# Attention scores in three single PSUM tiles, transposes in three banks

## The chip, the core and the metric

The kernel runs on one core of one Trainium2 chip. A core has a matrix engine (PE, with its weight loads, PEld), a vector engine (DVE), a scalar engine (ACT), a general engine (POOL) and queues that start transfers (SP, and POOL's own). PE writes its results into PSUM, which has eight banks; a bank holds 512 float32 numbers in each of 128 partitions, and DVE and ACT read them from there. The metric is the time on the device for one execution, in microseconds; lower is better.

## The reference

Eight batches with eight heads of 64 numbers each: 512 local and 32 global tokens. Local queries see the local keys within a window of 32 to either side, and all global keys; global queries see all keys. The result of the attention is the input of a layer of eight experts, where each token goes to one expert.

```python
s_g = scale * np.matmul(q_g, k_all.transpose(0, 1, 3, 2))
out_g = np.matmul(sm(s_g), v_all)
s_ll = np.where(mask, scale * np.matmul(q_l, k_l.transpose(0, 1, 3, 2)), -1e9)
s_l = np.concatenate([s_lg, s_ll], axis=-1)
out_l = np.matmul(sm(s_l), np.concatenate([v_g, v_l], axis=2))
...
expert_idx = np.argmax(logits, axis=1)
h = np.maximum(x[mask] @ w1[e], 0.0)
out[mask] = gate_w[mask, None] * (h @ w2[e])
```

## The kernel before

The kernel has an attention part, which also routes each token to its expert and scatters its row into a buffer in device memory (`xs`), and an expert part, which works through items of 128 rows of one expert.

**The attention part** is cut into steps, five for each batch. A batch has four *units* of 128 local queries (`unit`) and one *globals* piece of work (`globals_`). A unit is spread over three steps:

- `scores` (step t): 16 or 32 products of queries and keys (L439 for paired units, in which two heads' halves share a product; L443 for the others). On the chip each product is two instructions, so a unit is 32 instructions of L439 or 64 of L443. They fill two banks of PSUM, `s_ps[0]` and `s_ps[1]`, with four blocks k of 128 columns each. Then DVE reads the blocks, the two banks in turn (k = 0 of one, k = 0 of the other, and so on, L450): it adds the mask, writes the sum to `pb` and keeps the row maximum in `nm`. ACT takes the exponential of each block (L455). So there are eight reads and eight exponentials of 128x128 for a unit.
- `turn` (step t + 1): for each of two halves a tile `pt` (one bank) takes four transposes of `pb` (L463), and ACT copies it to `pT` (L464).
- `values` (step t + 2): 32 products with the values into the tile `po` (L474), and DVE's division by the row sum (L397 to L399, `quotients`) into `xt`, the attention's output.

The globals do the same with 544 keys in two parts (`scores(0, ...)` and `scores(1, ...)`, L513, L518, read by DVE in L529), then `turn` (L549 to L554) and `values` (L564).

The routing (`route`) works on the finished rows: it transposes them into `pt` tiles (`turn`, L594, copied by ACT in L596), multiplies with the experts' vectors (`logits`, L616, copied in L617 to `us`), transposes back (`back`, L635), finds the expert and the row's place (`choose`, `gates`, `place`, L687 to L709), and scatters the rows with indirect transfers on POOL's queue (`send`, L716).

**Buffers.** PSUM's eight banks in this part are three pools: `ps_s` for the scores (two tiles of two banks), `ps_o` for values (one tile of two banks), and `ps_t` for transposes and all the small products of the routing (two tiles of one bank, name `pt`). A pool hands its tiles out in turn; the first writer of a tile waits until the last reader of what lay there before is done. When the attention part is over, the pools are closed, and the expert part has four pools of its own over the same banks.

**Order.** The first steps (before step 2) and the last ones (from step 40) run in the order in which they are written. Between them a planner orders each engine's instructions when the program is built: among those whose inputs, by its own reckoning, are there and whose tile is free, it takes the one that is written first. What comes out of it is a fixed order on each engine, which the chip keeps to.

**Loads.** SP starts the transfers of queries, keys (`raw`) and values (`vt`) for the next batch, each tied to an instruction of the attention (`mark`, `paced`).

**The early block.** At the end of the attention two blocks of 128 rows of expert 0 are worked through outside of the items (`early_block`); the first of them runs between the last attention steps, takes its intermediate tiles (L154, L168) from `ps_s` and its last one (L181) from `ps_o`, both through short functions that hand out a tile (`acc`, `acc2`).

## Time and profile before

| | |
|---|---|
| median of 3 runs | 757.07 us (756.87 to 760.34) |
| the profiled execution: time | 755.93 us |
| the profiled execution: span from first to last instruction | 754.1 us |
| attention part | up to about 265 us |
| granted TensorE clock over the span | 0.993 |

The profile is that of one execution. In a list of groups, a row names the line, the engine, the operation, output and inputs by the names in the program, the shape and the count. In the timeline, a row is a run of like instructions: its start, its length, and in brackets the idle time of the engine before it with what ended it. In the list of waits, a row names who waited, for whom, the total, the number of times and the longest. "issue" stands where the profile shows nothing that the engine waited for. A wait for several things is put down to the one that came last by the profile.

### The profile page before, as it was taken

The numbers are of one execution on the slowest core, as the hardware profiler recorded it, in microseconds if no ns is written. First come the engines' busy times: TensorE is split into PE (matmuls) and PEld (weight loads), VectorE is DVE, ScalarE is ACT, GpSimd is POOL, SyncE is SP. The second block draws the span as 40 slices with busy tenths as digits, with TensorE's granted clock in tenths as the row PEclk, the third lists the DMA queues.
The fourth block names the chain that finished last, engine by engine and source line by source line (L and its number), as shares of the span: only waits on it lengthen the run. The fifth ranks groups of instructions, "written<-read, shape, count | busy, mean of one in ns | idle before, by whom it ended". The sixth has DMA issues, their size and how long they took to land.

```text
span 754.1 us, 23074 instructions
## 1 busy us (share of the span) xinstructions
PE 713.8 (95%) x7782; PEld 549.9 (73%) x7782; DVE 407.7 (54%) x1385; ACT 472.5 (63%) x988; POOL 289.2 (38%) x306
## 2 busy tenths in 40 slices
PE   8898998999989999999999999999999999999992
PEld 4576776666758546888888888888888888888882
DVE  2757666776665474454545454545555454544441
ACT  4767676766767545666666656565656565656661
POOL 1121241323312244544444444444444444445451
PEclk9999999999999999999999999999999999999997
DMA  9987878868865469566555556565656565556561
GB/s 290 353 272 244 270 219 254 250 205 272 244 219 170 129 248 328 199 220 209 211 203 217 194 222 209 211 210 210 207 199 218 203 210 204 209 206 218 198 225 65
DMA packets 67850, 166.69 MB, mean 221 GB/s; under 512 B 6532, under 2 KB 20484, under 8 KB 67728
## 3 DMA queue, kind: packets, MB, share of 16 engines
q1 hardware_dynamic: 61968, 147.25, 58.0%
q0 software_dynamic: 5760, 17.87, 6.8%
q8 instruction: 70, 1.15, 0.6%
q14 instruction: 52, 0.43, 0.2%
HBM read 142.49 MB, written 23.65 MB: 220 GB/s over the span
## 4 chain that ended last, share of the span: by engine, by line
PE 81%; ACT 5%; DVE 4%; issue 4%; DMA 3%; SPq 1%; POOL 0%; DVEq 0%; POOLq 0%; ACTq 0%
PE g L1085 18%; PE g L1081 18%; PE g L1080 18%; PE s_ps L439 4%; PE hps L1103 4%; ACT pb L455 4%; PE pt L463 3%; PE po L474 3%; PE pt L594 2%; PE po L564 2%; PE xps L1056 2%; DMA raw<-in_qk_dram 2%; PE s_ps L443 1%; PE s_ps L513 1%; DVE pb L450 1%
## 5 line engine op out<-in xcount | busy, mean ns | idle before, releaser
L1076 DVE TENSOR_TENSOR WL<-stg,WH 128x512 f32 (+1 forms) x144 | 151.9, 1055 | 129.6 <-ACT WH L1074 129.6
L1076 POOL TENSOR_TENSOR WL<-stg,WH 128x512 f32 (+1 forms) x144 | 174.1, 1209 | 93.6 <-ACT WH L1074 92.0
L1074 ACT CAST WH<-stg 128x512 f32 (+1 forms) x288 | 177.4, 618 | 7.0 <-DMA stg<-in_wraw_dram 2.9
L1080 PE MATMUL g<-WH,hH 128*128 (+1 forms) x288 | 120.0, 417 | 0.0
L1080 PE MATMUL g<-WH,xH 128*128 (+1 forms) x288 | 117.3, 407 | 0.0
L1085 PE MATMUL g<-WH,xL 128*128 (+1 forms) x288 | 114.2, 397 | 0.0
L1081 PE MATMUL g<-WL,xH 128*128 (+1 forms) x288 | 114.2, 396 | 0.0
L1081 PE MATMUL g<-WL,hH 128*128 (+1 forms) x288 | 113.9, 396 | 0.0
L455 ACT ACTIVATE pb<-pb,nm 128x128 f32<-128x128 f32 x256 | 78.9, 389 | 43.1 <-DVE nm L450 36.2
L139 POOL DMA_INDIRECT out_dram<-ob x37 | 36.8, 993 | 153.6 <-ACT ob L137 153.6
L1085 PE MATMUL g<-WH,hL 128*128 (+1 forms) x288 | 84.7, 395 | 0.0
L1106 DVE TENSOR_TENSOR hL<-hps,hH 128x512 fp32r<-128x512 f32 x72 | 49.8, 692 | 57.8 <-ACT hH L1105 57.8
L450 DVE CUSTOM_DVE_ANT_0 pb<-s_ps,mask 128x128 f32<-128x128 f32 x256 | 57.6, 285 | 43.3 <-PE s_ps L443 18.7
L716 POOL DMA_INDIRECT xs<-xt,si x32 | 32.0, 1000 | 88.2 <-DVE ss L600 19.9
L1085 PEld LDWEIGHTS g<-WH,hL 128*128 128x128 f32 x288 | 54.4, 189 | 13.1
L1085 PEld LDWEIGHTS g<-WH,xL 128*128 128x128 f32 x288 | 54.1, 188 | 13.0
L1097 ACT ACTIVATE h<-g 128x512 f32<-128x512 f32 x72 | 42.9, 596 | 32.7 <-PE g L1085 32.7
L137 ACT ACTIVATE ob<-g,xr 128x512 f32<-128x512 f32 x36 | 24.7, 687 | 61.1 <-PE g L1085 61.1
L1080 PEld LDWEIGHTS g<-WH,xH 128*128 128x128 f32 x288 | 54.3, 189 | 12.0 <-issue 0.2
L1081 PEld LDWEIGHTS g<-WL,xH 128*128 128x128 f32 x288 | 54.4, 189 | 11.7 <-DVE ob L138 0.2
L420 POOL COPY stg<-raw 64x512 f32<-64x512 f32 x42 | 26.5, 631 | 91.7 <-DMA xs<-xt,si 36.2
L1081 PEld LDWEIGHTS g<-WL,hH 128*128 128x128 f32 x288 | 54.4, 189 | 10.0
(199 smaller groups left out, 1054.8 us busy)
## 6 DMA issues: line engine op xcount, KB each, us to landing
stg<-in_wraw_dram SPq DMA_DIRECT2D x36, 2048.0 KB
vt<-in_va_dram SPq DMA_DIRECT2D x98, 260.0 KB
raw<-in_qk_dram SPq DMA_DIRECT2D x56, 204.0 KB
xr<-xs SPq DMA_DIRECT2D x38, 257.0 KB
raw<-in_qk_dram SPq DMA_DIRECT2D x28, 200.0 KB
xs<-fill SPq DMA_DIRECT2D x9, 514.0 KB
stg<-in_wraw_dram SPq DMA_DIRECT2D x16, 256.0 KB
vt<-in_va_dram SPq DMA_DIRECT2D x4, 520.0 KB
```

Of the source, the lines that this page charges most:

```text
L139: nc.gpsimd.indirect_dma_start(out=out[:, :], out_offset=bass.IndirectOffsetOnAxis(ap=ob[:, DM : DM + 1].bitcast(U32), axis=0), in_=ob[:, ...
L439: nc.tensor.matmul(s_ps[j // 2][rows2(j), cs], qd[:, k, j], ks, start=True, stop=True)
L450: ins = nc.vector.tensor_tensor_reduce(p1, s_ps[grp][:, cs], mask[:, m : m + P], -ISQ, 3.0e38, ALU.add, ALU.min, n1)
L455: nc.scalar.activation(p1, p1, AF.Exp, bias=n1, scale=-1.0)
L716: ins = nc.gpsimd.indirect_dma_start(out=xs[:, :], out_offset=bass.IndirectOffsetOnAxis(ap=st["si"][:, t : t + 1], axis=0), in_=get(t), in ...
L1074: made.append(nc.scalar.copy(WH[:, ds(ra, 1), cs], s3))
L1076: made.append(eng.tensor_tensor(WL[:, ds(r, 1), cs], s3, WH[:, ds(r, 1), cs], ALU.subtract))
L1080: reads.append(nc.tensor.matmul(o.unsqueeze(1), a, WH2[:, ds(rp, 1), sl], start=first, stop=False))
L1081: reads.append(nc.tensor.matmul(o.unsqueeze(1), a, WL2[:, ds(rp, 1), sl], start=False, stop=False))
L1085: reads.append(nc.tensor.matmul(o.unsqueeze(1), a, WH2[:, ds(rp, 1), sl], start=False, stop=last))
L1097: nc.scalar.activation(h[:, nh * 512 : (nh + 1) * 512], g, AF.Relu)
L1106: nc.vector.tensor_tensor(hL[:, nh * 4 : nh * 4 + 4, :].rearrange("p c n -> p (c n)"), hp_, hv, ALU.subtract)
```

## The change

The pool of the scores has three tiles of one bank (it had two tiles of two banks), and the pool of the transposes has three tiles (it had two). A unit, and each part of the globals, takes two single tiles where it took one double tile and split it. The early block takes a single tile where it took the first half of a double one. In all, the attention part has eight banks as before: 3 + 2 + 3 in place of 4 + 2 + 2.

```diff
-        ps_s = actx.enter_context(tc.tile_pool(name="ps_s", bufs=2, space=PSUM))
+        ps_s = actx.enter_context(tc.tile_pool(name="ps_s", bufs=3, space=PSUM))
         ps_o = actx.enter_context(tc.tile_pool(name="ps_o", bufs=1, space=PSUM))
-        ps_t = actx.enter_context(tc.tile_pool(name="ps_t", bufs=2, space=PSUM))
+        ps_t = actx.enter_context(tc.tile_pool(name="ps_t", bufs=3, space=PSUM))
...
             def scores():
                 raw = state["raw", b]
-                s_ps = ps_s.tile([P, 2, 512], F32, name="s_ps")
-                s_ps = [s_ps[:, grp] for grp in range(2)]
+                s_ps = [ps_s.tile([P, 512], F32, name="s_ps") for _ in half]
...
                     st["gm"] = sm.tile([P, 4], F32, name="gm")
-                s_ps = ps_s.tile([P, 2, 512], F32, name="s_ps")
-                s_ps = [s_ps[:, grp] for grp in range(2)]
+                s_ps = [ps_s.tile([P, 512], F32, name="s_ps") for _ in half]
                 kn = 96 * (w1 - w0)
...
-                lambda: ps_s.tile([P, 2, 512], F32, name="s_ps")[:, 0],
+                lambda: ps_s.tile([P, 512], F32, name="s_ps"),
                 lambda: ps_o.tile([P, 2, 512], F32, name="po")[:, 0],
```

## The prediction

> **What bounds the kernel now.** I read the page's table of engines first, then busy time by stretch.

> ```profile
> span 754.1 us, 23074 instructions
> PE 713.8 (95%) x7782; PEld 549.9 (73%) x7782; DVE 407.7 (54%) x1385; ACT 472.5 (63%) x988; POOL 289.2 (38%) x306
> ...
> 20.00:57.00 37.00, 31.96 (x842) 23.45 (x830) 23.97 (x150) 25.14 (x69) 7.27 (x14) 1.00 0.93 310
> 57.00:86.40 29.40, 27.42 (x670) 20.52 (x670) 20.04 (x125) 21.14 (x58) 8.34 (x13) 1.00 0.78 236
> 86.40:115.80 29.40, 27.20 (x670) 20.41 (x670) 20.39 (x125) 21.32 (x58) 9.26 (x14) 1.00 0.84 264
> ...
> 209.00:246.00 37.00, 33.97 (x860) 25.29 (x860) 24.13 (x152) 25.34 (x66) 8.06 (x15) 1.00 0.61 190
> ...
> 286.00:754.00 468.00, 453.77 (x2169) 368.32 (x2167) 227.29 (x291) 284.67 (x506) 210.85 (x181) 0.99 0.59 207
> ```

> The columns of a stretch are its length, then PE, weight loads, DVE, ACT and POOL. The pools that change live only in the attention part, up to some 265 us; the expert items after it have pools of their own. One batch of attention lasts 29.4 us, in which PE is busy 27.2 to 27.4 and ACT and DVE 20 to 21. So PE sets the pace, and the change adds or removes no instruction of it. What it can win is PE's idle time, about 2 us of a batch. The next question is what that idle time waits for: the list of waits of PE, 0 to 290 us (total, times, longest).

> ```profile
> PE s_ps L443 <- issue: 5.7, 6, 1.7
> PE pt L635 <- ACT pT L464: 4.7, 5, 1.1
> PE po L474 <- issue: 2.9, 6, 1.0
> PE s_ps L439 <- issue: 2.3, 1, 2.3
> PE pt L594 <- DVE xt L399: 1.9, 2, 1.2
> ...
> PE po L474 <- DVE nm L450: 1.1, 1, 1.1
> ...
> PE pt L549 <- ACT gT L550: 0.7, 1, 0.7
> ...
> PE pt L616 <- ACT pT L464: 0.5, 1, 0.5
> PE pt L463 <- ACT xT L596: 0.2, 1, 0.2
> ```

> Two things are to be seen. Transposes into `pt` wait for ACT's copies out of other `pt` tiles, 4.7 + 0.7 + 0.5 + 0.2 = 6.1 us in all. And no row has a matmul into `s_ps` waiting for DVE: with four banks the scores never stand behind a read. The rows with "issue" name no releaser, and I leave them as they are on both sides.

> **The change, part by part.**

> *Transposes get a third bank.* This is the wait at its most frequent place, by the timeline:

> ```profile
> 111.66 0.37 ACT L617 COPY us<-pt 128x256 f32<-128x256 f32 x1 [0.28 <-PE pt L616]
> 112.54 1.09 PE L463 MATMUL pt<-ident,pb 128*128 128x128 f32 x8
> 113.09 2.46 ACT L455 ACTIVATE pb<-pb,nm 128x128 f32<-128x128 f32 x8 [1.07 <-DVE nm L450]
> 113.57 1.12 PE L474 MATMUL po<-vt,pT 128*32 128x65 f32 x64
> 114.62 0.68 PE L513 MATMUL s_ps<-raw 64*32 64x288 f32 x6
> 115.20 0.69 DVE L399 TENSOR_TENSOR xt<-po,rs 128x512 f32<-128x512 f32 x1
> 115.46 1.04 ACT L464 COPY pT<-pt 128x512 f32<-128x512 f32 x2
> 116.08 0.66 PE L635 MATMUL pt<-ident,us 128*128 128x128 f32 x4 [0.77 <-ACT pT L464]
> 116.57 0.64 PE L594 MATMUL pt<-ident,xt 128*128 128x128 f32 x4
> 117.14 0.70 PE L513 MATMUL s_ps<-raw 64*32 64x288 f32 x10
> ...
> L464 ACT COPY pT<-pt x64: 559/578/597, 14.9 to 248.2; 128x512 f32<-128x512 f32 x64
> ```

> L463 has filled both banks by 113.63. ACT does eight exponentials (2.46 us) before it copies the first bank out, at 115.46 + 0.58 = 116.04, and L635 starts at 116.08. Its own input `us` was ready at 112.03. With a third bank (the one that L617 emptied at 112.03) L635 runs in the idle time, right behind the six L513. But the L594 behind it still needs the bank that ACT frees at 116.04, and its `xt` is ready only at 115.20 + 0.69 = 115.89; so it starts at about 116.08 in place of 116.57. The gain is 116.57 - 116.08 = 0.49 us at each of the five places, not the whole 0.8 to 1.1 us: 2.45. What is late next is ACT's first copy again. The three single waits have other work behind them and go whole: L616 0.5, L549 0.7, L463 0.2 (that one in the written tail). Together 3.8 us; the ends are 0, where every wait only moves to the next instruction, and 6.1, where all go.

> [...]

> *Scores lose a bank: three singles for four.* A unit takes two of the three, so its second tile is the first tile of the unit before, free only when DVE has read that one for the last time. The reads alternate between the two tiles, so this is the seventh of eight. The question is whether PE gets there earlier. There are 27 places from 35 us on where a unit or a globals part follows a unit's eight reads; these are the first, two of the three tightest and the last (DVE's seventh read, then PE's next matmuls).

> ```profile
> 35.42 0.29 DVE L450 CUSTOM_DVE_ANT_0 pb<-s_ps,mask 128x128 f32<-128x128 f32 x1
> 36.00 0.43 PE L439 MATMUL s_ps<-raw,stg 128*64 128x128 f32 x2
> ...
> 55.50 0.28 DVE L450 CUSTOM_DVE_ANT_0 pb<-s_ps,mask 128x128 f32<-128x128 f32 x1
> 55.71 0.28 DVE L450 CUSTOM_DVE_ANT_0 pb<-s_ps,mask 128x128 f32<-128x128 f32 x1
> 55.73 0.69 PE L513 MATMUL s_ps<-raw 64*32 64x288 f32 x6
> ...
> 144.83 0.29 DVE L450 CUSTOM_DVE_ANT_0 pb<-s_ps,mask 128x128 f32<-128x128 f32 x1
> 145.12 0.68 PE L513 MATMUL s_ps<-raw 64*32 64x288 f32 x6
> ...
> 236.81 0.28 DVE L450 CUSTOM_DVE_ANT_0 pb<-s_ps,mask 128x128 f32<-128x128 f32 x1
> 238.50 0.65 PE L439 MATMUL s_ps<-raw,stg 128*64 128x128 f32 x6
> ```

> The seventh read ends 0.29 us before the next scores at the first place, 0.05 after at the second, at the same instant at the third and 1.41 before at the last. The other 23 lie between -0.05 and 1.44. So PE is behind DVE already, because it does a turn (L463, 1.09) and the values (L474, 1.12) between two units. I charge 0.15 us (one read's step is 0.21, 55.50 to 55.71) at the three tightest: 0.4 us. The ends are 0 and one such step at all 32 units, 32 x 0.21 = 6.7. If the cover went (turn and values no longer in between), queued behind the stalled matmul would be all of PE: the turn, the values and the route's transposes, then ACT's copies. The globals' second part and the next unit are alike: they start after the reads that they need.

> [...]

> *Early block and tail.* The early block's tiles come from the scores' pool, three single slots for two double ones. Among the nine waits of PE above none is of these lines (L154, L168), so: nothing; a loss here has no mechanism, as the slots increase, and a gain has no wait to come from.

> *Order.* Between the first two steps and the last ones, the order on each engine is drawn up by the planner when the kernel is built, which takes whatever has a free tile. So it will not be the order above. The trace can't show the new one. I bound it by the waits: beyond 6.1, at best the waits for L594 (1.9) and L474 on DVE (1.1) go too; at worst the 6.7 above.

> **Sum.** -3.8 + 0.4 = -3.4 us. Does it reach the end? From the chain of work that ended last:

> ```profile
> 254.07 1.93 PE s_ps L168 x4
> ...
> 267.86 1.29 POOL xs L716
> ...
> 285.63 6.15 DMA stg<-in_wraw_dram
> ```

> The chain goes from PE's last attention work through the last scatters to the first weights of the items, with no stretch that has its own clock, so 1 us earlier is 1 us at the end. The profiled execution took 755.93 us (span 754.1), which gives 752.5. It lies 0.9 below the lowest of the three timed runs; against their median of 757.07 the forecast is **753.7**.

> **The rivals.**

> *Nothing is won.* ACT is what L635 waits for, and each wait goes on to the next transpose; the 0.49 is given back at the L594 or L463 behind it. For: L594's bank and `xt` are ready just then. Against: L635 is 0.49 us of work that fits in the gap. Time 757.1.

> *More is won.* The planner, free of the two-bank limit, moves later work into the rest of the gaps: 3.4, plus 6.1 - 3.8 = 2.3, plus 1.9 + 1.1 = 8.7; time 748.4. For: weight loads are busy 20.5 of 29.4 us only, so PE's stream has room. Against: L594 waits for `xt`, which no bank makes earlier.

> *Slower: the scores stand behind DVE.* The planner draws turn or values out from between two units, PE reaches the shared bank before the seventh read, and DVE can't start the next unit either: scores and reads take turns. It decides from a margin under zero; two places are there already. At one read's step for each of 32 units, without any gain, 757.07 + 6.7 = 763.8. For: margins of 0.1 to 0.4 at half the places. Against: 1.4 us at many others, and ACT's 2.46 us of exponentials stay the longer leg.

> **How the numbers follow.** Forecast 0.46 (751.3 to 756, nearly even about the bound of faster), nothing won 0.16, more 0.18, slower 0.20. A measurement of this kernel tells about 0.5% from no change: 753.3 to 760.9. Faster: 0.22 of the forecast and 0.18: 0.40. Slower: 0.17 of its case. Same: 0.24 + 0.16 + 0.03 = 0.43. The range must take in most of the rivals on both sides: 748 to 763, which leaves out some 0.05 below and 0.1 above.

> **What would show it.** Right: the rows "L635 <- ACT pT L464" are gone from PE's waits, a batch is 0.5 us shorter, and no row of `s_ps` waiting for `nm L450` adds up to over 1 us. Wrong: such a row at several us; or L594 or L463 waiting for ACT in L635's place with the batch at 29.4. The items' 468 us should stay; a change there would make the argument wrong from the start, as would a PE order in which units follow each other without a turn in between.

## The result, and the profile after

The changed kernel takes 745.13 us (median of 4 runs, 744.32 to 746.92) against 756.97 us (4 runs, 756.02 to 760.34) beside it: a ratio of 0.984, 95% interval 0.980 to 0.987. Two later series of it gave 745.7 and 745.39 us, ratios 0.983 [0.981, 0.985] and 0.983 [0.979, 0.986]. So the kernel is faster by 1.6%, 12 us. The forecast had the sign, with 753.7 us, but the time lies under the range's lower end of 748: the gain is 3.5 times the one forecast.

Line numbers of the changed kernel are smaller by one from the scores on and by two from the globals' scores on: L439 is now L438, L443 is L442, L463 is L462, L464 is L463, L474 is L473, L513 is L511, L594 is L592, L616 is L614, L635 is L633. First the head and the engines, then the busy time by stretch (length, PE, weight loads, DVE, ACT, POOL, granted clock, DMA share, GB/s).

```profile
span 743.4 us, 23099 instructions
...
PE 704.2 (95%) x7779; PEld 554.8 (75%) x7782; DVE 404.5 (54%) x1385; ACT 469.8 (63%) x988; POOL 289.3 (39%) x306
```

```profile
20.00:57.00 37.00, 32.76 (x837) 25.83 (x826) 24.61 (x161) 25.81 (x71) 7.28 (x14) 0.95 0.92 304
57.00:86.40 29.40, 26.76 (x669) 21.22 (x668) 19.17 (x124) 20.80 (x57) 8.35 (x13) 0.94 0.82 254
86.40:115.80 29.40, 27.17 (x744) 22.46 (x747) 21.42 (x137) 22.38 (x60) 8.80 (x14) 1.00 0.88 269
```

PE's busy time fell from 713.8 to 704.2 us, with the same matmuls: 9.6 of the 10.7 us that the span lost. In the stretch from 86.4 to 115.8 PE is busy as long as before (27.17 against 27.20) and gets 744 matmuls done instead of 670. Single stretches differ with the groups that fall into them; over all the time up to 209 us PE is busy for 187.70 us against 188.43, with 4697 matmuls against 4476. Idle time is not what was won. The list of waits of PE up to 290 us (total, times, longest) says the same:

```profile
PE po L473 <- issue: 7.0, 9, 2.6
PE s_ps L442 <- issue: 6.8, 4, 2.5
PE pt L550 <- issue: 2.0, 1, 2.0
...
PE pt L592 <- DVE xt L399: 0.8, 1, 0.8
PE pt L592 <- ACT pT L463: 0.4, 1, 0.4
```

The waits of transposes for ACT's copies are gone but for 0.4 us, and no row has scores waiting for `nm`. But the stalls with no releaser ("issue") have grown. So the question is why the same matmuls keep PE busy for less time. The groups of PE show where, for 20 to 290 us (line, operation, tiles, shapes and count; then busy time in us, mean ns of one; then idle before). The kernel before, then the changed one:

```profile
L439 PE MATMUL s_ps<-raw,stg 128*64 128x128 f32 x672 | 51.6, 279 | 2.3 <-issue 2.3
...
L513 PE MATMUL s_ps<-raw 64*32 64x192 f32 (+1 forms) x256 | 18.5, 374 | 0.0
```

```profile
L438 PE MATMUL s_ps<-raw,stg 128*64 128x128 f32 x672 | 46.2, 283 | 0.0
...
L511 PE MATMUL s_ps<-raw 64*32 64x288 f32 (+1 forms) x256 | 11.9, 374 | 0.0
```

The same 672 and 256 matmuls, each as long as before by the mean, keep PE busy for 5.4 and 6.6 us less, 12.0 in all. Matmuls overlap (672 of 279 ns one behind the other would be 187 us, and they are 51.6), so the busy time of a group is the length of its runs; many short runs are longer than a few whole ones. The timeline of PE (start, length, then the group) shows the runs. One unit before:

```profile
97.44 1.30 PE L439 MATMUL s_ps<-raw,stg 128*64 128x128 f32 x18
98.68 0.64 PE L549 MATMUL pt<-ident,gp 128*96 128x128 f32 x4
99.25 0.64 PE L616 MATMUL pt<-xT,en 128*32 128x256 f32 x8
99.82 0.66 PE L439 MATMUL s_ps<-raw,stg 128*64 128x128 f32 x8
100.41 0.66 PE L594 MATMUL pt<-ident,xt 128*128 128x128 f32 x4
101.00 0.65 PE L439 MATMUL s_ps<-raw,stg 128*64 128x128 f32 x6
101.58 1.09 PE L463 MATMUL pt<-ident,pb 128*128 128x128 f32 x8
```

and after:

```profile
103.02 1.97 PE L438 MATMUL s_ps<-raw,stg 128*64 128x128 f32 x32
104.92 1.09 PE L462 MATMUL pt<-ident,pb 128*128 128x128 f32 x8
...
112.91 0.72 PE L511 MATMUL s_ps<-raw 64*32 64x288 f32 x16
113.55 1.09 PE L462 MATMUL pt<-ident,pb 128*128 128x128 f32 x8
```

From start to start, the 32 score matmuls take 1.24 + 0.59 + 0.58 = 2.41 us in three pieces (97.44 to 98.68, 99.82 to 100.41, 101.00 to 101.58), and 104.92 - 103.02 = 1.90 us in one: 0.25 us for each cut. Six take 0.58 and 32 take 1.90, so by these two each matmul adds (1.90 - 0.58) / 26 = 0.051 us, and what is left, some 0.27 us, is paid once a run. That is a rough line: the eight at 99.82 take 0.59, and it gives 0.68. With the globals the length hardly counts. Sixteen in one run take 113.55 - 112.91 = 0.64 us. The prediction itself quoted ten of them from 117.14 before; the next row there is this:

```profile
117.77 0.66 PE L463 MATMUL pt<-ident,pb 128*128 128x128 f32 x4
```

So those ten took 117.77 - 117.14 = 0.63 us, as long as sixteen; the run of six ahead of them, 0.68 us by its row, came on top. Of the 21 units of L439 one is whole in the kernel before, and 14 in the changed one.

To count this over the whole attention I added up, over PE's records from its first matmul to the last scores on `stg`, the time from the start of one matmul to the start of the next. Idle time of over 0.15 us goes to its releaser; the rest is "change" if line or tiles differ between the two, "within" if not. In us (the number of changes in brackets), with the time of the profiled execution. The expectations below count changes of line in the program as it was built, which gives fewer (299 and 252 for these two).

| kernel | profiled time | total | at changes | within | named waits | issue |
|---|---|---|---|---|---|---|
| before | 755.93 | 240.1 | 58.8 (341) | 160.5 | 10.1 | 10.7 |
| after | 745.14 | 229.6 | 46.9 (284) | 163.2 | 2.6 | 16.9 |

PE's attention ends 10.5 us earlier: 11.9 less at changes, 7.5 less in named waits, 6.2 more in stalls without a releaser, 2.7 more within. The chain that ended last carries it on: the first weights of the items start at 274.58 (285.63 before), and from there to the end it is 743.4 - 274.58 = 468.8 us against 468.5. The items did not change.

```profile
256.90 1.29 POOL xs L714
...
274.58 6.42 DMA stg<-in_wraw_dram
```

### The profile page after: what moved, and what is told of

It reads as the page before. It is cut to its first block, busy times and chain, and to the rows that moved or that the text cites. A ratio compares the mean times of both kernels' runs of the same rounds, so it can differ in the third digit from the quotient of the medians.

```text
span 743.4 us, 23099 instructions
## 1 busy us (share of the span) xinstructions
PE 704.2 (95%) x7779; PEld 554.8 (75%) x7782; DVE 404.5 (54%) x1385; ACT 469.8 (63%) x988; POOL 289.3 (39%) x306
## 3 DMA queue, kind: packets, MB, share of 16 engines
q1 hardware_dynamic: 61968, 147.25, 58.9%
## 4 chain that ended last, share of the span: by engine, by line
PE 85%; issue 4%; DVE 3%; DMA 3%; SPq 2%; ACT 1%; POOL 1%; DVEq 0%; POOLq 0%; ACTq 0%
PE g L1083 18%; PE g L1079 18%; PE g L1078 18%; PE s_ps L438 5%; PE hps L1101 4%; PE po L473 4%; PE pt L462 4%; PE pt L592 3%; PE xps L1054 2%; PE po L562 2%; PE s_ps L442 2%; DMA raw<-in_qk_dram 1%; PE s_ps L511 1%; PE pt L614 1%; PE pt L547 1%
## 5 line engine op out<-in xcount | busy, mean ns | idle before, releaser
L449 DVE CUSTOM_DVE_ANT_0 pb<-s_ps,mask 128x128 f32<-128x128 f32 x256 | 57.3, 286 | 32.9 <-PE s_ps L442 20.2
L1078 PEld LDWEIGHTS g<-WH,hH 128*128 128x128 f32 x288 | 54.3, 189 | 9.7
```

Source lines behind the costliest of these rows:

```text
L449: ins = nc.vector.tensor_tensor_reduce(p1, s_ps[grp][:, cs], mask[:, m : m + P], -ISQ, 3.0e38, ALU.add, ALU.min, n1)
L1078: reads.append(nc.tensor.matmul(o.unsqueeze(1), a, WH2[:, ds(rp, 1), sl], start=first, stop=False))
```

## The experiments

**The theories.** A: the third bank for transposes lets the planner keep a unit's scores together, and PE's stream gets shorter because it has fewer changes of kind. B: the split of the scores' double tiles into singles does it. C: three banks for scores cost something, because scores stand behind DVE's reads. There are two more rivals of A: D, that the bank wins at run time what the waits cost, whatever the order, and E, which came later, that changes of kind cost nothing by themselves.

**One part alone: singles for the scores, transposes with two banks again.** Three banks for scores, then four.

```diff
-        ps_t = actx.enter_context(tc.tile_pool(name="ps_t", bufs=3, space=PSUM))
+        ps_t = actx.enter_context(tc.tile_pool(name="ps_t", bufs=2, space=PSUM))
```

> Scores in three single tiles, transposes with two banks as before. The built PE order has 300 changes of line in the attention, as before has (299), against 252 after the change. Theory A (the third transpose bank lets the planner leave groups of matmuls whole, and each change of group on PE costs some 0.16 us): no gain, 756 to 758. Rival B (the split of the double tile into singles frees banks sooner): 745 to 750. Rival C (three banks make scores stand behind DVE's reads): 760 or more, with rows of s_ps waiting for nm L449 of several us. Waits of L633 on ACT's copies of about 4 to 6 us stay under A.

> Scores in four single tiles, transposes with two banks: the banks of before, only handed out one by one. 299 changes of line. Theory A: 756 to 758, the same as the run with three singles. Rival B: 745 to 750. Rival C: 757, and so faster than the run with three singles by 3 us or more.

With three banks: 755.99 us (10 runs, 752.37 to 762.35), ratio 0.999 [0.995, 1.004]. With four (`ps_s` with `bufs=4` as well): 754.3 us (10 runs, 751.99 to 756.53), ratio 0.996 [0.994, 0.998]. Of the first, a row of the waits and two of the groups:

```profile
PE pt L633 <- ACT pT L463: 3.6, 6, 0.7
```

```profile
L438 PE MATMUL s_ps<-raw,stg 128*64 128x128 f32 x672 | 53.0, 283 | 2.0 <-issue 2.0
...
L511 PE MATMUL s_ps<-raw 64*32 64x288 f32 (+1 forms) x256 | 19.4, 374 | 0.0
```

Both the waits for ACT's copies and the long busy times (53.0 and 19.4) are back. B falls, but for some 0.4% that four singles win and three do not. C is small: between three banks and four lie 0.3%, with intervals that overlap. From three singles with two banks for transposes to the changed kernel it is one bank more, and on that bank the gain hangs.

**Whole groups by hand, with two banks and with three.** PE runs in the order in which the program is written, in which nothing cuts a unit; the other engines stay with the planner. The same edit on the kernel before (`before_pe`) and on the changed one (`after_pe`):

```diff
-        emit(2, t - 2)
+        with tc.manual_schedule(engines={ENG.PE}):
+            emit(2, t - 2)
```

> The pools of before, but PE's instructions of the planned steps stand in the written order: 241 changes of line against 299, no more banks. Theory A: 58 changes x 0.16 = 9.3 us less, so 745 to 750, with waits for ACT's copies out of pt still there. Rival D (the gain comes from the run-time waits that the third bank removes, the order does nothing): 757 or more.

> The pools of after with PE in the written order: the same PE order as the run before this one. Theory A: 11 changes fewer than after, 743 to 745; the distance to the run with the pools of before is what the banks are worth at run time, at most the 6 us of waits for copies out of pt. Rival D: 6 us or more under the run with the pools of before, and 751 or so.

With two banks 817.23 us, ratio 1.080 [1.076, 1.084]; with three 750.61 us (745.2 to 754.36), ratio 0.992 [0.987, 0.997]. The expectation for two banks was wrong by far: I had taken the cut groups for a loss that could simply be undone. With three it was missed too (743 to 745): named waits take 10.6 us there against 2.6 in the changed kernel, so the order with every unit whole is not the best one. The waits of the two-bank kernel up to 350 us, and one of them in the timeline:

```profile
PE pt L549 <- ACT gT L550: 21.2, 8, 2.8
PE pt L635 <- ACT pT L464: 17.3, 7, 2.6
PE pt L616 <- ACT pT L464: 15.2, 6, 3.3
```

```profile
61.82 1.09 PE L463 MATMUL pt<-ident,pb 128*128 128x128 f32 x8
...
62.38 2.44 ACT L455 ACTIVATE pb<-pb,nm 128x128 f32<-128x128 f32 x8 [4.46 <-DVE nm L450]
64.73 1.04 ACT L464 COPY pT<-pt 128x512 f32<-128x512 f32 x2
...
65.35 0.66 PE L635 MATMUL pt<-ident,us 128*128 128x128 f32 x4 [2.43 <-ACT pT L464]
```

The turn (L463) fills both banks; ACT has eight exponentials of the next unit ahead of the copies, and PE, held to its order, waits 2.43 us. So the cuts of the kernel before were a way round these waits: while ACT is busy, PE does pieces of the next scores and slips the other transposes in as banks come free. With the pools of the change the same written order costs 66.6 us less. That is what they are worth to an order of whole groups; the planner, with them, leaves 14 of the 21 units whole.

**The dose: more changes, nothing else.** `dose0` is `after_pe` with a unit's values right behind its turn; `dose2` lets turn and values alternate in quarters in 18 units. The other engines have the same order in both; PE has 108 more changes of line (349 against 241 in the program's order). From `dose0` to `dose2`, in batches 1 to 6 (`turn` and `values` are also rewritten to take a quarter `q`, which is not shown):

```diff
-                at(t + 1, turn, 1)
-                at(t + 2, values, 1.15)
+                for q in range(4):
+                    at(t + 1, lambda q=q: turn((q,)), 1 + q / 30)
+                    at(t + 2, lambda q=q: values((q,)), 1.01 + q / 30)
```

> Pools of after, PE in the written order, and the values of a unit moved up to stand right behind the turn of the next one: 241 changes of line. All theories: like the run with pools of after in the written order, 744 to 752. It is the measure for the next run.

> As the run before, but in 18 units turn and values alternate in quarters (two transposes, 16 instructions of values, and so on): 349 changes of line against 241, the same instructions, the same order on every other engine, the same banks. Theory A': a change of group costs PE 0.10 to 0.16 us whatever the banks: 108 of them make 11 to 17 us more. Rival E (the many changes in before only stand where PE would have waited anyway and cost nothing by themselves): within 3 us of the run before.

756.4 us (12 runs, 750.97 to 760.79) and 765.02 us (6 runs, 762.61 to 766.93), ratios 0.997 [0.994, 0.999] and 1.008 [1.006, 1.010]. The groups that were cut, in `dose0` and in `dose2` (values L474 of the kernel before, then the turn L463; the edit moves the lines), for 20 to 300 us:

```profile
L473 PE MATMUL po<-vt,pT 128*32 128x65 f32 x2048 | 39.3, 223 | 6.4 <-issue 6.4
L462 PE MATMUL pt<-ident,pb 128*128 128x128 f32 x241 | 33.9, 284 | 0.0
```

```profile
L481 PE MATMUL po<-vt,pT 128*32 128x65 f32 x2044 | 48.9, 226 | 3.5 <-issue 3.4
...
L466 PE MATMUL pt<-ident,pb 128*128 128x128 f32 x240 | 45.5, 297 | 0.0
```

The busy time of the same work grows by 9.6 and 11.6 us. Changes and within together grow by 17.3 us (from 208.5 to 225.8), 0.16 us for each of the 108. Of that the total grows by 10.6 and the median time by 8.6 us, because the stalls without a releaser fall by 8.1 (14.4 to 6.3) while named waits rise by 1.4. E falls, though the 8.6 us are less than the 11 to 17 that A' had. `dose0` itself took longer than expected (744 to 752): named waits are 18.9 us there, among them 3.0 in four waits of scores for DVE's reads (L442 behind `gm`). A change costs, then; and part of what it costs, or saves, is offset in the stalls without a releaser.

**Two banks for scores, four for transposes,** and with it the route's transposes written right behind a unit's turn:

```diff
-        ps_s = actx.enter_context(tc.tile_pool(name="ps_s", bufs=3, space=PSUM))
+        ps_s = actx.enter_context(tc.tile_pool(name="ps_s", bufs=2, space=PSUM))
...
-        ps_t = actx.enter_context(tc.tile_pool(name="ps_t", bufs=3, space=PSUM))
+        ps_t = actx.enter_context(tc.tile_pool(name="ps_t", bufs=4, space=PSUM))
...
-                at(t0 + 3 + t, turn(t), 3)
+                at(t0 + 3 + t, turn(t), 1.05)
```

> Scores in two single tiles, transposes in four banks: 242 changes of line. Theory A': 10 changes fewer than after, 1 to 2 us less, and almost no wait left for copies out of pt: 742 to 746 if after is at 745. Rival C (scores stand behind DVE's reads, which with two banks holds for both tiles of a unit): 750 or more, with rows of s_ps waiting for nm L449.

> Two banks for scores and four for transposes, and the route's transposes written right behind the unit's turn (due 1.05 in place of 3), so that transposes follow transposes: 138 changes of operand shape where the changed kernel has 165 and the 2-and-4 split alone 155. By the cost of 0.1 to 0.17 us of a change that is 1.7 to 2.9 us under the 749.8 of the 2-and-4 split: 747 to 748, and no better than the changed kernel unless the stalls at PE's code blocks, which the split had more of (12.7 us against 6.8 at L442), come down too; then 742 to 744. If changes of shape cost nothing by themselves: 750.

749.8 us, ratio 0.989 [0.986, 0.992], without the last edit; 747.66 us, ratio 0.986 [0.983, 0.990], with it. They spend less time at changes than the changed kernel (44.8 and 42.2 us against 46.9) and are not faster; the first was expected at 742 to 746. Nor do scores wait for DVE, even with two banks, but for one wait of 0.5 us in the first. The head of the waits of the second:

```profile
PE s_ps L442 <- issue: 12.5, 7, 3.6
PE po L473 <- issue: 10.8, 17, 3.1
```

Stalls without a releaser come to 20.2 and 22.9 us against 16.9: what the order saves comes back there, and in the first of them in 4.6 us more within groups as well. I found no version that beats the changed kernel.

**The bank without the order.** The changed kernel's pools, with PE held to exactly the order of the kernel before (`seq` is that order, by instruction numbers); POOL and SP have the same order too, ACT and DVE nearly.

```diff
         emit(2, t - 2)
+        for lo, hi in zip(seq, seq[1:]):
+            tc.add_manual_dep(
+                nc.find_inst_by_name(f"I-{hi}"),
+                f"I-{lo}",
...
```

> The pools of the change, but PE held to the kernel before's own order of instructions, its 299 changes of line and 87 groups of scores with it; POOL and SP have the same order too, ACT and DVE nearly. So only the third bank's effect at run time is left, the one that the prediction priced. By the theory that the order carries most of the gain, the waits of transposes for ACT's copies go (6.1 us in the kernel before) and the rest stays: 751 to 754, PE's changes of line still cost some 52 us between the first and the last scores on stg, and the waits of L633 for the copy L463 are gone. By the rival that the bank itself carries it, 745 to 747. By the rival that at this order the bank is worth nothing because the next transpose waits in its place, 756 to 757.

> The changed kernel once more, as the measure for the three runs beside it on the same chip: 12 us under before, ratio 0.984.

> The changed kernel again, beside the run in the old order on the same chip: 744 to 747.

759.23 us (12 runs, 755.12 to 764.5), ratio 1.002 [0.9995, 1.005]; on the same chip the changed kernel took 745.39 us, ratio 0.983 [0.979, 0.986]. The pools are the same, so the order is worth all of the gain; PE's above all, though ACT's and DVE's orders differ between the two runs as well. I had expected 751 to 754: the bank alone should have won its waits, and it won nothing. The waits of transposes for ACT's copies did go but for 0.5 us, as the list of waits shows, and 1.9 us of waits of scores for DVE's reads (`nm`, `gm`) are new; below it the score groups:

```profile
PE po L473 <- issue: 7.0, 7, 3.7
PE s_ps L442 <- issue: 6.9, 4, 2.4
PE pt L551 <- issue: 1.7, 1, 1.7
...
PE s_ps L511 <- DVE nm L449: 1.0, 1, 1.0
...
PE s_ps L511 <- DVE gm L527: 0.9, 1, 0.9
...
PE pt L592 <- ACT pT L463: 0.5, 1, 0.5
```

```profile
L438 PE MATMUL s_ps<-raw,stg 128*64 128x128 f32 x672 | 53.0, 285 | 0.0
...
L511 PE MATMUL s_ps<-raw 64*32 64x192 f32 (+1 forms) x256 | 19.8, 374 | 1.9 <-DVE nm L449 1.0 <-DVE gm L527 0.9
```

The groups are as long as in the kernel before. To see whether the lost gain was an accident of one profile, both kernels ran once more, one execution each:

> The kernel before once more, for a second profile. If the split of PE's time is a property of the order and the banks: from the start to the last scores on stg some 10.7 us of stalls with no releaser (issue), 9 us behind ACT and DVE, 160 us within groups; the time 755 to 760.

> The changed pools in the old order once more, for a second profile. If the waits that the third bank takes away come back as stalls with no releaser and a lower clock: ACT and DVE together under 3.5 us (the kernel before has 9), issue 14 to 18 us (it has 10.7), the time 756 to 762. If the first profile was an accident: issue 9 to 12 us, the granted clock 1.00 in all stretches, the time 751 to 754.

| kernel | profiled time | total | at changes | within | named waits | issue |
|---|---|---|---|---|---|---|
| before | 755.93 | 240.1 | 58.8 | 160.5 | 10.1 | 10.7 |
| before_again | 752.29 | 237.2 | 58.9 | 158.7 | 9.8 | 9.7 |
| s3_t2 | 755.39 | 241.1 | 59.9 | 161.8 | 8.5 | 10.9 |
| s4_t2 | 752.54 | 236.9 | 59.9 | 160.6 | 7.2 | 9.2 |
| frag | 759.16 | 244.2 | 59.7 | 164.8 | 3.5 | 16.3 |
| frag_again | 757.91 | 243.6 | 60.1 | 163.6 | 3.2 | 16.7 |
| after | 745.14 | 229.6 | 46.9 | 163.2 | 2.6 | 16.9 |
| after_third | 742.87 | 229.0 | 46.0 | 163.9 | 2.7 | 16.4 |
| s2_t4 | 750.11 | 235.3 | 44.8 | 167.8 | 2.4 | 20.2 |
| s2_join105 | 747.32 | 232.5 | 42.2 | 163.6 | 3.8 | 22.9 |
| dose0 | 756.37 | 241.8 | 44.8 | 163.7 | 18.9 | 14.4 |
| dose2 | 766.93 | 252.4 | 63.7 | 162.1 | 20.3 | 6.3 |
| before_pe | 816.10 | 298.2 | 50.8 | 174.5 | 67.8 | 5.1 |
| after_pe | 749.82 | 235.9 | 44.5 | 163.9 | 10.6 | 16.9 |

It was none. In both pairs the named waits lose some 6.5 us, the stalls without a releaser gain 5.6 to 7.0, and 4 to 5 us more are spent within groups. From `frag` to after, with one set of pools, the total falls by 14.6 us, 12.8 of it at changes.

## Why the prediction was wrong

- *What bounds the kernel.* PE sets the pace: right. "The change adds or removes no instruction of it. What it can win is PE's idle time, about 2 us of a batch": wrong. Busy time was no fixed sum per instruction: 9.6 us of it went with not one matmul less. The sign was in the rows quoted: weight loads are busy 20.5 of 29.4 us where PE is busy 27.4. In these two traces PE's busy share does not tell the kernels apart, 95% on both sides, while that of weight loads rises from 73 to 75%.
- *Transposes' third bank, -3.8.* The waits went as said, all of them rather than part: L635 behind ACT from 4.7 to nothing, and ACT's from 6.1 to 0.4. But their time was not won: the run in the old order has a ratio of 1.002. The step "1 us earlier is 1 us at the end" holds behind the attention, and fails inside it, where the stalls without a releaser grow by 5.6 to 7.0 us. So the forecast's sign came out right by another mechanism than its own, which is luck.
- *Scores' ring, +0.4,* an estimate from the margins of before, where no scores waited for a read. Nothing in the changed kernel. In the old order, at which it was priced, there is the row of 1.0 us (L511 behind `nm` L449), at one of the places of this kind; for a term of 0.4 with ends of 0 and 6.7 that is near. But the globals' second part, which it put at nothing ("they start after the reads that they need"), waits 0.9 us there (L511 behind `gm` L527).
- *Early block and tail, 0.* Right, as far as the chain shows (468.5 and 468.8 us from the first weights on). The list of waits of before does have rows of L154 and L168, which the quoted excerpt leaves out; they come to 1.7 us before and 1.8 after.
- *Order.* This is the step that failed. "It will not be the order above. [...] I bound it by the waits": the new order was bounded by what could be won of idle time, 8.7 us at most, though the rows in hand had scores in pieces of 6 and 10. The order is worth 14 us at equal pools (759.23 to 745.39); in the profiles, 12.8 of 14.6 us are less time at changes of kind.
- *The rivals.* "More is won" came nearest in time (748.4), by another mechanism: the gaps it would have filled are not where the gain is. "Nothing is won" names the right time for the bank alone, but the waits went into stalls without a releaser rather than on to the next transpose. "Slower" did not happen: in the changed kernel no scores wait for DVE, and with two single banks for scores there is one wait of 0.5 us. In other orders such waits do come (1.9 us in `frag`, 3.0 in `dose0`).
- *What would show it.* The rows of L635 are gone and no row of `s_ps` behind `nm` is there, both as forecast; yet a batch became shorter by some 1.5 us (10.5 us over seven batches) instead of 0.5. The signs asked for could not tell the forecast's mechanism from the real one; a row of groups with its busy time would have.

Shown: the gain needs the third bank of the transposes (`s3_t2`, `s4_t2`), it comes through the order (`frag` against after), by the table through PE's changes of kind, and extra changes cost time with all else equal (`dose2`). That the planner cut the groups for want of a bank is inferred from what whole groups cost with two (`before_pe`); its reckoning is not to be seen in a trace. The new order with two banks was not run.

## What to carry to other kernels

Where a planner sets the order, ask of a buffer first which order it forbids, and only then which wait it ends. Compare a group's busy time with the length of one unbroken run of the same matmuls in the timeline: what is over that is the price of cuts, here 0.16 to 0.25 us each, and more for the globals' scores (0.68 + 0.63 us in two runs against 0.64 in one), and it hides in an engine that looks 95% busy. And do not count a wait that is taken away as won: here, with the order held still, 6.5 us of named waits went, 5.6 to 7.0 us of stalls without a releaser came, and the ratio was 1.002. Test it so.

## What the runs showed of the hardware

**Stalls at fixed places of PE's stream.** Nearly all stalls without a releaser of over 0.5 us in the attention lie at fixed places of the stream whatever the order: counted over all records of PE (matmuls, weight loads, register and semaphore instructions), in the runs of the old order at 451, 707, 1475, 2755, 4035, 5314, 6595, 6850, 8131 and 9410, which lie multiples of 256 apart, to within one. In `before_again` and `frag_again` the one at 2755 lasts 0.49 and 1.41 us, that at 5314 1.32 and 2.47: longer where PE comes with fewer waits, though not at every place (1.80 and 1.71 at 9410). The longest of all, 3.7 us, is the one at 1475 in `frag`.

**The clock after a stall.** Stretches of the changed kernel behind the stall of 2.52 us that ends at 120.76:

```profile
121.00:122.00 1.00, 1.00 (x31) 0.62 (x16) 0.12 (x1) 0.00 (x0) 0.00 (x0) 0.50 0.61 227
122.00:123.00 1.00, 1.00 (x6) 0.97 (x6) 1.00 (x11) 0.78 (x3) 0.00 (x0) 0.50 0.09 33
...
125.00:126.00 1.00, 1.00 (x49) 0.91 (x38) 0.36 (x2) 1.00 (x3) 0.00 (x0) 1.00 0.96 326
```

```profile
121.77 1.09 PE L547 MATMUL pt<-ident,gp 128*96 128x128 f32 x4
```

The granted clock is 0.50 for 3.4 us, and four transposes take 1.09 us instead of the 0.64 of L549 x4 above. The traces show four such periods of 3.4 us in the changed kernel's attention, which start 0.1 to 1.4 us behind the ends of stalls of 2.62, 1.82, 2.52 and 2.47 us (at 37.55, 65.84, 120.76 and 206.12), 10.2 us in all in `frag` and in `frag_again`, and none in the kernel before in either profile. That fits the additional time within groups (2.7 us, 4.3 and 4.9); that it is all of it is not shown. The lower clock does not follow every stall: behind one of 2.32 us in the kernel before (it ends at 38.75) the clock stays at 1.00, and so it does behind one of 2.05 us in the changed one (at 93.94). Nor does it go by the length of the stall here: 1.82 us had the lower clock behind them and 2.32 us had not.
